# Folding the sub-key weights of a product-key expert layer: unreduced 32-bit products in two column tiles, the folded pieces kept on chip

## The chip, the cores and the metric

One core of a Trainium2 chip runs the kernel. The metric is the device time of one execution in microseconds (us). TensorE multiplies matrices, VectorE (DVE) and ScalarE (ACT) work on elements, GpSimd (POOL) too, and SyncE (SP) issues nearly all transfers, in the order of the program. Each engine takes its own instructions in order and waits on semaphores for the others. All data in fast memory lie in 128 partitions; products land in PSUM, in banks of 512 32-bit numbers for each partition.

## What is computed

Attention with 16 heads, and then a layer of experts that are found by product keys, each behind a layer norm and with a residual sum. N is 2048 tokens, D = 448.

```python
h  = x + attention(layernorm(x), wqkv, wo)
xf = layernorm(h)
q  = einsum("nd,dhc->nhc", xf, w_q)           # 16 heads, 2 x 256
s1 = einsum("nhd,ed->nhe", q[..., :256], k1)  # 64 sub-keys
s2 = einsum("nhd,ed->nhe", q[..., 256:], k2)
# the 8 best of each, the 8 best of their 64 sums, softmax g over these, for each head
act = gelu(einsum("nd,nhkd->nhk", xf, u[top_e]))
out = h + einsum("nhk,nhk,nhkd->nd", g, act, v[top_e])
```

The scores s1 and s2 depend on xf only through products of w_q with the sub-keys. The kernel forms those products once (the *folding*: for each head a matrix of 448 x 128, 64 columns for k1 and 64 for k2), and later multiplies xf with the folded matrix.

## The kernel before

**Stages.** First the layer norm and the projections to q, k and v (up to about 152 us). Then attention in 256 steps; a step u takes one block of 128 keys for four heads and 512 queries. Beside its steps run the folding, the preparation of u and v, and for three of the four blocks of 512 tokens the output projection (`project`) and the search for the best sub-keys (`search`). After it (from about 925 us) come the experts.

**Order.** The order of every engine's instructions is the program's. `weave` (L163) lays generators side by side: each gets a number of turns and a stretch, in attention steps, and the one whose next turn is due first goes next. So a stretch (1, 59) with 48 turns has one turn in 1.21 steps. What a function puts into `due` is issued at the next `flush` (L179), at the latest in the next attention step.

**An attention step.** `scores` issues twelve products for S, two steps ahead, and ScalarE takes two exponentials (L530). `values` (L546) multiplies V with the exponentials in four column tiles of 32, unreduced 32-bit on both sides, into the accumulator A. There is one bank named A: after 16 steps (u = 15, 31, ...) VectorE copies it out (L557), and the next accumulation may begin. Three steps later `finish` (L533) transposes the copy in four products (L540) and VectorE divides by the sums (L542, L543). Every fourth step, after its products with V, `load_kv` (L206) loads K and V for a group of four steps two groups later (L201, L213). There is also only one bank named M; the folding, `finish`, `project` and `search` all take it in turn.

**The folding** (class `Fold`, L225). The sub-keys are split into a high and a low part in the 32-bit form with reduced products, 64 columns each, side by side (`kk`). For each head h and half f, VectorE casts the raw weights to a high part (L252), and VectorE (f = 0) or GpSimd (f = 1) subtracts for the low part (L254). `fold` issues four products of 448 columns (through the helper at L90): two contraction tiles by the high and low part. VectorE copies the lower 64 rows out (L266) and adds the upper ones (L267), and fills the last 64 columns (L269). `flip` transposes the head's matrix in four products (L277), ScalarE copies it out (L279), and at the next flush VectorE takes the largest magnitude (L139 by `see`) and SP stores the piece to the slow memory (L283). Raw weights are loaded four heads ahead (L242), into eight buffers. That is three turns for a head.

**Scales and halves.** The folded weights, u and v are scaled by a power of two from their largest magnitude and split into two 16-bit parts, a pair that is called halves below. For u and v, `tops` (L969) loads each of 32 tiles and takes its maximum two turns later. `share` (L141) reduces the maxima (L142), writes 128 numbers to the slow memory (L144), reads them back for all partitions (L146), and VectorE reduces them (L149) and forms the scale. `part` (L982) then loads a tile (L984), makes its halves (for the folded weights on VectorE, L159 and L991; for u and v on GpSimd, L993 to L997) and stores them (L1000). The halves of two parts have five buffers, which u and the folded weights share.

**The stretches**, in attention steps of the whole: folding 1 to 59; maxima of u 1 to 25; scale of u 26 to 33; halves of u 33 to 59 (14 tiles) and 64 to 110 (18); scale of the folded weights 60 to 65, their halves 65 to 87; wo loaded 60 to 68; projections from 67, 131 and 195, each followed by its search 26 steps on; maxima of v 87 to 110, its scale 111 to 116, its halves 118 to 170 and 170 to 240.

Of the kernel before, what the change touches and what calls it, by code (L numbers as in the profile page):

```python
# [58 lines left out]
def block(ctx: ExitStack, tc: tile.TileContext, x, wqk, wv, wo, wq, k12, uT, v, cst, out):  # L59
# [4 lines left out]
    v_d = dram.tile([4, 4, 128, 4, 128], F32, name="vd")  # L64
    wr_d = [dram.tile([128, 4, 128], F32, name=f"wr{h}") for h in range(H)]
    wp_d = [dram.tile([128, 2, 4, 4, 128], F16, name=f"wp{i}") for i in range(4)]
# [156 lines left out]
    class Fold:  # L223


        def __init__(self, rawp):
            self.rawp = rawp
            kr = rawp.tile([128, 2, 2, 64], F32, name="kr", bufs=1)
            nc.sync.dma_start(kr, k12)
            self.kk = kk = rawp.tile([128, 2, 2, 128], FR, name="kk", bufs=1)  # L230
            nc.vector.tensor_copy(kk[:, :, :, :64], kr)
            nc.vector.tensor_tensor(kk[:, :, :, 64:], kr, kk[:, :, :, :64].bitcast(F32), op=OP.subtract)
            self.raw = {}
            for h in range(4):
                self.load(h)
# [9 lines left out]
        def run(self, pool, psum):  # L245

            parts, wts = {}, {}

            def parts_of(h, f):
                w = self.raw[h][f]  # L250
                wh = pool.tile([128, 2, D], FR, name="wqh", bufs=4)
                nc.vector.tensor_copy(wh, w)  # L252
                wl = pool.tile([128, 2, D], FR, name="wql", bufs=4)
                (nc.gpsimd if f else nc.vector).tensor_tensor(wl, w, wh.bitcast(F32), op=OP.subtract)  # L254
                parts[h, f] = wh, wl

            def fold(h, f):
                pf = psum.tile([128, 512], F32, name="M")
                hl = parts.pop((h, f))
                mm_all(pf[:, :D], [(self.kk[:, f, kt], r[:, kt]) for kt in range(2) for r in hl])  # L260

                def add():
                    if not f:
                        wts[h] = pool.tile([128, 512], F32, name="wt")
                    lo = pool.tile([64, D], F32, name="lo", bufs=1)
                    nc.vector.tensor_copy(lo, pf[64:, :D])  # L266
                    nc.vector.tensor_tensor(wts[h][64 * f:64 * f + 64, :D], pf[:64, :D], lo, op=OP.add)  # L267
                    if f:
                        nc.vector.tensor_copy(wts[h][:, D:], wts[h][:, 384:D])  # L269

                due.append(add)

            def flip(h):
                wt = wts.pop(h)
                pt = psum.tile([128, 4, 128], F32, name="M")
                for t in range(4):
                    nc.tensor.transpose(pt[:, t], wt[:, 128 * t:128 * t + 128], ident)  # L277
                of = pool.tile([128, 4, 128], F32, name="of")
                nc.scalar.activation(of, pt, AF.Copy)  # L279

                def store():
                    WS.see(h, of.rearrange("p t c -> p (t c)"))
                    nc.sync.dma_start(wr_d[h], of)  # L283

                due.append(store)

            parts_of(0, 0)
            parts_of(0, 1)
            for h in range(H + 1):
                for f in range(2):  # L290
                    if h < H:
                        flush()
                        fold(h, f)
                        if h + 1 < H:
                            parts_of(h + 1, f)
                            if f:
                                self.raw.pop(h)
                                self.load(h + 4)
                        yield
# [682 lines left out]
    def part(S, src, dst, cols, planes):  # L982
# [5 lines left out]
        r, h = raw[:, :cols], [hl[:, k, :cols] for k in range(planes)]  # L988
        if S is WS:
            times(h[0], r, S.scale)  # L990
            nc.vector.scalar_tensor_tensor(h[1], r, S.scale, h[0], op0=OP.mult, op1=OP.subtract)  # L991
        else:
            nc.gpsimd.tensor_scalar(r, r, S.scale, 1.0, op0=OP.mult, op1=OP.mult)  # L993
            nc.gpsimd.tensor_copy(h[0], r)
            nc.gpsimd.tensor_tensor(h[1], r, h[0], op=OP.subtract)
            if planes == 3:
                nc.gpsimd.tensor_scalar(h[2], h[0], 1.0 / LS, 1.0, op0=OP.mult, op1=OP.mult)  # L997
        yield
# [11 lines left out]

    def parts_of_folded():
        return pipeline([part(WS, wr_d[h].rearrange("p t c -> p (t c)"),
                              wp_d[h // 4][:, :, h % 4].rearrange("p f t c -> p f (t c)"), 512, 2) for h in range(H)], 1)

    def scales():
# [4 lines left out]
        yield  # L1020

    with tc.manual_schedule(engines={ET.PE, ET.DVE, ET.Activation, ET.Pool, ET.SP}):
# [24 lines left out]
        wol = wo_p.tile([128, 4, D], FR)  # L1047
        work = [(a, 197, 0, 197), (load_wo(), 5, 0, 8)]
        for b in range(3):
            t = 64 * b + 7  # L1050
            look = search(b, [(i, j) for g in ((0, 1), (2, 3)) for i in range(4) for j in g])
            work += [(project(b), PROJECT, t, t + PROJECT), (islice(look, 1), 1, t + 22, t + 23)]
            t += 26
            work += [(look, SEARCH, t, t + SEARCH)]
            if b < 2:
                work += [(chain(*[pairs_of(j, nc.gpsimd) for j in range(4)]), 4 * PAIRS_POOL, t + 18, t + 82),
                         (places_of(b, nc.scalar), PLACES, t + 82, t + 94)]
            else:
                work += [(pipeline([pairs_of(j, nc.gpsimd) for j in (0, 1)], 6), 6 + PAIRS_POOL, t + 20, 197)]
# [182 lines left out]
```

## Time and profile before

| | |
|---|---|
| median of three runs | 1704.33 us (1703.49 to 1708.09) |
| the profiled execution | 1696.69 us |
| its span, first to last instruction | 1694.9 us |
| mean granted clock of TensorE | 0.984 |
| moved by transfers | 301.32 MB, mean 178 GB/s |

In the rows that follow, a group names the line, the engine, the operation, what is written and read, the shape and the count; behind the bar stand the busy time in us and the mean of one in ns, then the idle time of the engine just before, and what ended it. A row of the chain has a start, a length and what it was spent on: the work of an engine, a transfer, or the issue of one on SP's queue (SPq). A row of a window has the stretch, its length, and the busy time of the engine with the count of instructions, then the granted clock, the share of the transfer engines and GB/s. A row of waits has the total in us, the count and the longest.

### The profile page before, as it was taken

Reading aid. Unit: us, or ns where it says so; the run is one execution under the profiler, and the core shown is the slowest. Engines: PE = TensorE matmul, PEld = TensorE weight load, DVE = VectorE, ACT = ScalarE, POOL = GpSimd, SP = SyncE. Lnnn points to the kernel's source line nnn. Section 1 sums busy time; section 2 is a strip of 40 time slices with the busy share of each in tenths; the row PEclk is TensorE's granted clock in tenths of the full one; section 3 lists DMA queues with packets and bytes.
Section 4 is the critical chain, followed back from the end, with each engine's and each line's share of the span. In section 5 each row is a group of like instructions: output and inputs, shape, how many; then the busy total and the mean of one; then the engine's idle time right before and its main releaser. Section 6 shows DMA issues by size and latency. Waiting matters only on the chain.

```text
span 1694.9 us, 33544 instructions
## 1 busy us (share of the span) xinstructions
PE 1598.7 (94%) x12577; PEld 811.4 (48%) x12577; DVE 1254.8 (74%) x3907; ACT 896.7 (53%) x1272; POOL 421.1 (25%) x514
## 2 busy tenths in 40 slices
PE   6999898987899999999998899899999999999999
PEld 5776343443333443344333564445544554555544
DVE  6654866456587658857678899968999799779832
ACT  3545666775677877688775344233432344333322
POOL 3452115634414663267534200000000000000000
PEclk9999999998999999999999999999999999999999
DMA  8755958678984666455752324445434443554354
GB/s 262 258 193 182 300 196 273 223 244 262 337 293 137 204 224 191 157 178 181 252 174 80 94 83 136 142 125 147 125 115 138 150 130 101 153 152 130 107 146 134
DMA packets 164356, 301.32 MB, mean 178 GB/s; under 512 B 15328, under 2 KB 63584, under 8 KB 164192
## 3 DMA queue, kind: packets, MB, share of 16 engines
q1 hardware_dynamic: 159968, 297.07, 55.7%
q10 hardware_dynamic: 4224, 2.10, 0.4%
q8 instruction: 99, 1.62, 0.4%
q14 instruction: 65, 0.53, 0.1%
HBM read 237.24 MB, written 61.87 MB: 176 GB/s over the span
## 4 chain that ended last, share of the span: by engine, by line
PE 62%; DVE 24%; DMA 8%; issue 2%; POOL 1%; ACT 1%; SPq 0%; DVEq 0%; POOLq 0%; ACTq 0%
PE acc L1157 15%; PE M L90 10%; PE A L90 9%; PE A L552 9%; PE S L526 9%; PE pq L90 6%; DVE p L932 4%; DVE ti L762 2%; DVE G L953 2%; DMA raw<-in_uT_dram 2%; DVE fg L917 2%; DVE pos L789 2%; DMA raw<-in_v_dram 1%; DVE ti L761 1%; PE A L959 1%
## 5 line engine op out<-in xcount | busy, mean ns | idle before, releaser
L530 ACT ACTIVATE P<-S 128x1024 f32<-128x1024 f32 x512 | 495.9, 1022 | 134.8 <-PE S L526 133.5
L1157 PE MATMUL acc<-v,w 128*128 128x448 f16 x1536 | 306.0, 353 | 0.0
L526 PE MATMUL S<-qS,kS 32*128 32x512 f32 x3072 | 267.0, 432 | 5.2 <-ACT P L530 4.5
L552 PE MATMUL A<-P,V 128*32 128x512 f32 x2048 | 267.8, 613 | 3.4 <-DVE o L557 3.4
L526 PEld LDWEIGHTS S<-qS,kS 32*128 32x128 f32 x3072 | 140.5, 186 | 161.6 <-issue 96.9
L1157 PEld LDWEIGHTS <-w 128*128 128x128 f16 x1536 | 149.0, 98 | 141.7 <-issue 1.4
L90 PEld LDWEIGHTS <-u 128*128 128x128 f16 x1408 | 133.5, 98 | 151.7 <-issue 11.1
L1131 ACT ACTIVATE w<-ring 128x512 f16<-128x512 f32 x128 | 80.5, 630 | 205.4 <-PE acc L1157 106.6
L932 DVE TENSOR_TENSOR p<-st,iota 128x2048 f16<-128x2048 f16 x128 | 156.4, 1222 | 7.7 <-PE A L959 4.1
L90 PE MATMUL A<-XHb,u 128*128 128x512 f16 x568 | 138.5, 388 | 4.5 <-DVE G L953 4.0
L90 PE MATMUL M<-w,XHb 128*128 128x512 f16 x512 | 129.8, 384 | 7.4 <-DMA w<-wp 3.1
L1132 DVE SCALAR_TENSOR_TENSOR w<-w,ring 128x512 f16<-128x512 f16 x128 | 87.2, 686 | 66.2 <-ACT w L1131 66.2
L1130 DVE SCALAR_TENSOR_TENSOR ring<-ring,wscale,G 128x512 f32<-128x512 f32 x128 | 92.7, 744 | 34.6 <-ACT ring L1116 34.4
L90 PE MATMUL M<-XHb,u 128*128 128x512 f16 x456 | 110.9, 379 | 0.8 <-DVE G L953 0.8
L552 PEld LDWEIGHTS A<-P,V 128*32 128x32 f32 x2048 | 45.9, 109 | 108.2 <-issue 99.6
L813 POOL TENSOR_TENSOR sel<-sel,iv 128x256 f16<-128x256 f16 x80 | 54.0, 706 | 174.1 <-DVE sel L809 174.1
L1116 ACT ACTIVATE ring<-A,ugelu 128x512 f32<-128x512 f32 x71 | 48.5, 684 | 89.2 <-PE A L90 89.1
L761 DVE MAX8 ti<-fresh 128x8 f32<-128x64 f32 x384 | 80.6, 210 | 17.1 <-ACT fresh L739 17.0
L762 DVE FIND_INDEX8 ti<-ti,fresh 128x8 uint32<-128x64 f32 x384 | 84.2, 219 | 0.0
L1116 ACT ACTIVATE ring<-M,ugelu 128x512 f32<-128x512 f32 x57 | 39.2, 688 | 81.9 <-PE M L90 81.7
L90 PEld LDWEIGHTS <-XHb 128*128 128x128 f16 x512 | 45.4, 98 | 72.5 <-issue 21.3
L917 DVE TENSOR_TENSOR fg<-f,st 128x2048 f16<-128x2048 f16 x64 | 78.7, 1230 | 0.1
(197 smaller groups left out, 2325.7 us busy)
## 6 DMA issues: line engine op xcount, KB each, us to landing
v<-vs SPq DMA_DIRECT2D x128, 336.0 KB, 2.9
kS<-ks SPq DMA_DIRECT2D x64, 512.0 KB, 5.5
u<-us SPq DMA_DIRECT2D x128, 256.0 KB, 2.7
w<-wp SPq DMA_DIRECT2D x56, 512.0 KB, 5.5
V<-vd SPq DMA_DIRECT2D x64, 256.0 KB, 3.1
raw<-in_uT_dram SPq DMA_DIRECT2D x64, 256.0 KB, 5.1
wr<-in_wq_dram SPq DMA_DIRECT2D x32, 448.0 KB, 6.3
raw<-in_v_dram SPq DMA_DIRECT2D x64, 224.0 KB, 5.3
```

The source lines that it names most:

```text
L90: nc.tensor.matmul(ps, l, r, start=i == 0, stop=i == len(pairs) - 1)
L526: nc.tensor.matmul(S[j // 2][:, j % 2], kS[r, a, 128 * (k % 4):128 * (k % 4) + 128], qS[r, c], start=m == 0, stop=m == 2)
L530: nc.scalar.activation(Pt[:, 2 * i:2 * i + 2], S[i], AF.Exp)
L552: nc.tensor.matmul(O[n][32 * j:32 * j + 32], V[:, k % 4, j], Pt[:, j], start=k == 0, stop=k == NT - 1)
L761: nc.vector.max(t8[:, 4 * i + k], src[:, 64 * k:64 * k + 64])
L762: nc.vector.max_index(i8[:, 4 * i + k], t8[:, 4 * i + k], src[:, 64 * k:64 * k + 64])
L917: nc.vector.tensor_tensor(fg.rearrange("p t k f u -> p t k (f u)"), f1.rearrange("p t f u -> p t (f u)").unsqueeze(2).to_broadcast([128, T ...
L932: newest[0] = nc.vector.tensor_tensor(p1, pairs(0, s, TG, 128), ids(TG, 128), op=OP.is_equal).ins
L1116: nc.scalar.activation(act, p, AF.Gelu_apprx_tanh, scale=ugelu)
L1130: nc.vector.scalar_tensor_tensor(av, av, wscale, of_expert(b, f), op0=OP.mult, op1=OP.mult)
L1132: nc.vector.scalar_tensor_tensor(w[:, 1], w[:, 0], -LS, a, op0=OP.mult, op1=OP.add)
L1157: nc.tensor.matmul(acc[j][:, :D], l, r, start=f == 0 and k == 0, stop=f == 31 and k == 2)
```

## The change

The raw weights and sub-keys are multiplied as they are, unreduced 32-bit on both sides. Each head has one turn with four products: two contraction tiles, and in each the two halves f as two column tiles of 64, into the two halves of one bank. No cast, no subtraction and no sum is left; VectorE copies the 128 x 448 out and fills the last 64 columns. A head takes two turns (fold, flip); the raw weights of head h + 4 are loaded right behind the fold of head h. ScalarE copies each flipped piece to a tile of its own, which stays; the store and the load of the pieces go. `Fold.parts` makes the halves from these tiles.

The first stretch of the weave grows from 60 to 66 steps. In it: folding 1 to 50 in 32 turns; then, in one chain, the scale of the folded weights and their halves, 51 to 66, in 21 turns; maxima of u as before; scale of u 26 to 32; the first 14 halves of u 32 to 66. Behind it, in steps of the whole: wo 66 to 71, the other 18 halves of u 66 to 106, maxima of v 72 to 132 (60 steps instead of 23), its scale 133 to 139, its halves 140 to 186 (14 tiles) and 186 to 246 (18). The first loads of each search come two steps earlier. Projections and searches stay where they were.

```diff
-            kr = rawp.tile([128, 2, 2, 64], F32, name="kr", bufs=1)
-            nc.sync.dma_start(kr, k12)
-            self.kk = kk = rawp.tile([128, 2, 2, 128], FR, name="kk", bufs=1)
-            nc.vector.tensor_copy(kk[:, :, :, :64], kr)
-            nc.vector.tensor_tensor(kk[:, :, :, 64:], kr, kk[:, :, :, :64].bitcast(F32), op=OP.subtract)
+            self.keys = rawp.tile([128, 2, 2, 64], F32, name="kr", bufs=1)
+            nc.sync.dma_start(self.keys, k12)
...
-            def fold(h, f):
+            def fold(h):
                 pf = psum.tile([128, 512], F32, name="M")
-                hl = parts.pop((h, f))
-                mm_all(pf[:, :D], [(self.kk[:, f, kt], r[:, kt]) for kt in range(2) for r in hl])
-
-                def add():
-                    if not f:
-                        wts[h] = pool.tile([128, 512], F32, name="wt")
-                    lo = pool.tile([64, D], F32, name="lo", bufs=1)
-                    nc.vector.tensor_copy(lo, pf[64:, :D])
-                    nc.vector.tensor_tensor(wts[h][64 * f:64 * f + 64, :D], pf[:64, :D], lo, op=OP.add)
-                    if f:
-                        nc.vector.tensor_copy(wts[h][:, D:], wts[h][:, 384:D])
+                w = self.raw.pop(h)
+                for kt in range(2):
+                    for f in range(2):
+                        nc.tensor.matmul(pf[64 * f:64 * f + 64, :D], self.keys[:, f, kt], w[f][:, kt],
+                                         start=kt == 0, stop=kt == 1)
+
+                def out():
+                    wts[h] = pool.tile([128, 512], F32, name="wt")
+                    nc.vector.tensor_copy(wts[h][:, :D], pf[:, :D])
+                    nc.vector.tensor_copy(wts[h][:, D:], pf[:, 384:D])
...
-                of = pool.tile([128, 4, 128], F32, name="of")
-                nc.scalar.activation(of, pt, AF.Copy)
-
-                def store():
-                    WS.see(h, of.rearrange("p t c -> p (t c)"))
-                    nc.sync.dma_start(wr_d[h], of)
+                of = pool.tile([128, 512], F32, name=f"of{h}", bufs=1)
+                nc.scalar.activation(of, pt.rearrange("p t c -> p (t c)"), AF.Copy)
+                self.folded.append(of)
+                due.append(lambda: WS.see(h, of))
...
-        STEPS = 3 * H
+        STEPS = 2 * H
+
+        def parts(self):
+
+            for h, of in enumerate(self.folded):
+                hl = sp.tile([128, 2, 512], F16, name="hl", tag="hl2", bufs=5)
+                times(hl[:, 0], of, WS.scale)
+                nc.vector.scalar_tensor_tensor(hl[:, 1], of, WS.scale, hl[:, 0], op0=OP.mult, op1=OP.subtract)
+                yield
+                nc.sync.dma_start(wp_d[h // 4][:, :, h % 4].rearrange("p f t c -> p f (t c)"), hl)
...
-        weave((islice(a, 60), 60, 0, 60), (fold[0].run(fold_p, P[0]), Fold.STEPS, 1, 59),
-              (tops(US, lambda f: uT[:, f].rearrange("p t e -> p (t e)"), 512), TOPS, 1, 25), (US.share(), 5, 26, 33),
-              (parts_of_up(0, 14), 14 + PART, 33, 59))
+        weave((islice(a, FOLDED), FOLDED, 0, FOLDED), (fold[0].run(fold_p, P[0]), Fold.STEPS, 1, 50), (chain(WS.share(), fold[0].parts()), 5 + H, 51, FOLDED),
+              (tops(US, lambda f: uT[:, f].rearrange("p t e -> p (t e)"), 512), TOPS, 1, 25), (US.share(), 5, 26, 32),
+              (parts_of_up(0, 14), 14 + PART, 32, FOLDED))
...
-        work += [(WS.share(), 5, 0, 5), (parts_of_folded(), H + PART, 5, 27), (parts_of_up(14, 32), 18 + PART, 4, 50),
-                 (tops(VS, lambda f: v[:, f], D), TOPS, 27, 50), (VS.share(), 5, 51, 56), (scales(), 1, 56, 57),
-                 (parts_of_down(0, 14), 14 + PART, 58, 110), (parts_of_down(14, 32), 18 + PART, 110, 180)]
+        work += [(parts_of_up(14, 32), 18 + PART, 0, 40), (tops(VS, lambda f: v[:, f], D), TOPS, 6, 66), (VS.share(), 5, 67, 73), (scales(), 1, 73, 74),
+                 (parts_of_down(0, 14), 14 + PART, 74, 120), (parts_of_down(14, 32), 18 + PART, 120, 180)]
```

More of the change, by code (lines that the diff above doesn't have):

```diff
@@ L277, in flip @@
                     nc.tensor.transpose(pt[:, t], wt[:, 128 * t:128 * t + 128], ident)
[L278 to L299 removed]
+                of = pool.tile([128, 512], F32, name=f"of{h}", bufs=1)
+                nc.scalar.activation(of, pt.rearrange("p t c -> p (t c)"), AF.Copy)
+                self.folded.append(of)
+                due.append(lambda: WS.see(h, of))
+            for h in range(H + 1):
+                if h < H:
+                    flush()
+                    fold(h)
+                    self.load(h + 4)
+                    yield
                 if h:
@@ L988, in part @@
         r, h = raw[:, :cols], [hl[:, k, :cols] for k in range(planes)]
[L989 to L997, printed above, removed]
+        nc.gpsimd.tensor_scalar(r, r, S.scale, 1.0, op0=OP.mult, op1=OP.mult)
+        nc.gpsimd.tensor_copy(h[0], r)
+        nc.gpsimd.tensor_tensor(h[1], r, h[0], op=OP.subtract)
+        if planes == 3:
+            nc.gpsimd.tensor_scalar(h[2], h[0], 1.0 / LS, 1.0, op0=OP.mult, op1=OP.mult)
         yield
@@ L1020, in scales @@
         yield
+    FOLDED = 66
     with tc.manual_schedule(engines={ET.PE, ET.DVE, ET.Activation, ET.Pool, ET.SP}):
```

24 lines of the change are left out of this document (7 added, 17 removed).

## The prediction

> **What bounds the kernel now.** I read the page first, then a table of stretches for the exponentials of the attention, then the chain of waits, the groups by shape, and the waits of SP's queue.
>
> ```profile
> PE 1598.7 (94%) x12577; PEld 811.4 (48%) x12577; DVE 1254.8 (74%) x3907; ACT 896.7 (53%) x1272; POOL 421.1 (25%) x514
> PE 62%; DVE 24%; DMA 8%; issue 2%; POOL 1%; ACT 1%; SPq 0%; DVEq 0%; POOLq 0%; ACTq 0%
> ```
>
> The page shows TensorE busy for 94% of the span, but only 62% of the chain is its; VectorE holds 24% and transfers 8%. So TensorE is made to wait somewhere, and the change is worth what it does to those places. The next table finds them. Its rows are stretches in us; the count is that of exponentials, two to an attention step, so each stretch is known in steps (26, 24, 16, then six steps of the third again, 36, 24 and 36).
>
> ```profile
> core 0: us, ACT busy (x), PEclk, DMA share, GB/s
> 153.30:235.50 82.20, 50.39 (x52) 0.94 0.79 261
> 235.50:304.30 68.80, 46.53 (x48) 1.00 0.69 232
> 304.30:345.60 41.30, 31.02 (x33) 1.00 0.60 190
> 333.50:345.60 12.10, 11.62 (x13) 1.00 0.49 126
> 345.60:467.30 121.70, 69.70 (x72) 0.93 0.86 294
> 467.30:542.80 75.50, 46.52 (x48) 1.00 0.69 222
> 550.90:649.50 98.60, 69.69 (x72) 1.00 0.67 212
> ```
>
> A step with nothing beside it takes 12.1/6 = 2.02 us. Steps 66 to 102 (from 345.6) and their counterpart 64 steps later (from 550.9) issue the same work on TensorE, a projection and the start of a search, yet the first takes 121.7 us against 98.6: 23.1 us more, at a granted clock of 0.93 and a DMA share of 0.86. The folding runs beside steps 1 to 59, and its floor follows from the chain where nothing disturbs it:
>
> ```profile
> 288.85 0.59 PE M L277 x4
> 289.43 0.91 PE S L526 x11
> 290.34 0.99 PE A L552 x8
> 291.34 1.01 PE M L90 x4
> ...
> 310.99 0.67 PE M L540 x4
> ```
>
> A step is S and A, 1.90 us; a half fold (four products) adds 1.01, a flip (four transposes) 0.59. A head has two half folds and a flip in 58/16 = 3.625 steps: 2 x 2.91 + 2.49 + 0.625 x 2.02 = 9.57 us, 153.1 for 16. With two plain steps and three finishes of an accumulator (0.67 each, the last row) steps 0 to 60 would take 159 us. They took 192.3 - 12.1 = 180.2 (the first three rows less the fourth). So 21 us are stalls, about 13 of them in the first row: its floor is 25/3.625 x 9.57 + 2.0 + 0.7 = 68.7 of 82.2.
>
> **The change, part by part.** *Products.* Four products with 128 output columns per half become four products per head with 64, in unreduced 32-bit form. The nearest rows are V times P: unreduced too, four column tiles of 32.
>
> ```profile
> 461.11 1.85 PE A L552 x16
> L552 PE MATMUL A<-P,V 128*32 128x512 f32 x648 | 88.9, 621 | 1.7 <-DVE o L557 1.7
> ```
>
> A step has four such products and the trace shows eight instructions, so each product is two passes. Sixteen instructions in 1.85 us are four slots of 0.46 us in which the four tiles run side by side. For 448 columns a slot is 0.46 x 448/512 = 0.405 us; two contraction tiles by two passes make four slots if the two column tiles overlap: 1.62 us, and 0.07 at the edge (0.99 alone against 0.925 in the row of sixteen): 1.69 per head against 2.02. The trace has no column tile of 64, so both ends: 1.62 if they overlap, and 8 x 0.62 x 448/512 = 4.34 us if every pass waits for the one before and lasts as long as its record. I take 1.69, as the row of A is nearest. A faster order than A's is excluded, since passes into one half of the bank follow one another.
>
> The Trainium skill ("TensorE: Matmul & The Clock Gate", Part 3, The mechanism) says that matmuls start and end strictly in program order. If the two passes of a product stand side by side in that order, the second tile could begin only with the first one's second pass: five slots, 2.03 us per head, 6.5 us more. For A that would be five slots of 0.46 = 2.3 us a step; the trace has 0.99, so it speaks against it here.
>
> A head now has one fold and one flip in 49/16 = 3.06 steps: (1.90 + 1.69) + 2.49 + 1.06 x 2.02 = 8.22 us, 131.5 for 16. That is steps 1 to 50; with step 0, three finishes and 16 plain steps, steps 0 to 67 have a floor of 131.5 + 2.0 + 2.0 + 32.3 = 167.8, against 194.3 measured (192.3 and one plain step).
>
> *VectorE and GpSimd.* Per head the casts, one subtraction, the two copies and two sums go; the other subtraction leaves GpSimd (16 x 2.13 us, off the chain).
>
> ```profile
> L254 POOL TENSOR_TENSOR wql<-wr,wqh 128x896 fp32r<-128x896 f32 x16 | 34.0, 2127 | 112.5 <-DVE wqh L252 53.6 <-PE M L90 35.3 <-issue 17.5
> L266 DVE COPY lo<-M 64x448 f32<-64x448 f32 x32 | 20.0, 626 | 25.9 <-PE M L90 25.2
> L267 DVE TENSOR_TENSOR wt<-M,lo 64x448 f32<-64x448 f32 x32 | 19.7, 617 | 1.1
> L254 DVE TENSOR_TENSOR wql<-wr,wqh 128x896 fp32r<-128x896 f32 x15 | 19.4, 1295 | 0.5
> L252 DVE CAST wqh<-wr 128x896 fp32r<-128x896 f32 x29 | 19.2, 662 | 0.0
> L269 DVE COPY wt<-wt 128x64 f32<-128x64 f32 x16 | 7.4, 465 | 0.5
> L139 DVE TENSOR_REDUCE tops<-of 128x1 f32<-128x512 f32 x16 | 11.0, 685 | 24.0 <-ACT of L279 24.0
> L557 DVE COPY o<-A 128x512 f32<-128x512 f32 x5 | 3.4, 687 | 7.3 <-PE A L552 7.3
> ```
>
> Before: 2 x (0.63 + 0.62 + 0.66) + 1.30 + 0.47 + 0.69 = 6.3 us a head. After: one copy of 128 x 448 (not in the trace; 0.63 to 0.69 by the copies of 64 x 448 and 128 x 512), one of 64 columns and the maximum: 1.7 to 1.8. So 4.5 us a head, 72 us in all, leave an engine that is in order and whose evacuation of the one bank M is what the next fold or flip waits for.
>
> ```profile
> 169.86 6.62 DMA raw<-in_uT_dram
> ...
> wr<-in_wq_dram SPq DMA_DIRECT2D x32, 448.0 KB, 6.3
> ...
> SPq L283 <- ACT of L279: 53.3, 13, 6.4
> SPq L213 <- PE A L552: 36.6, 12, 8.5
> ```
>
> These are a row of the chain, one of the page's table of transfers and two of the waits of SP's queue between 153 and 330 us. The stalls of the first row begin here: tiles of u arrive late, the maximum over them holds VectorE, and the evacuation behind it holds TensorE. They arrive late because SP's queue stands still for the store of each folded piece (53.3 us). These stores go. In their place the load of head h+4 waits until TensorE has finished fold h, since the raw weights are now read there; behind it in SP's queue are its own 0.9 MB (two of 448 KB, 3.5 us at the 261 GB/s of the first row) and the next tiles of u, whose maxima VectorE then awaits, 3 to 4 us a head. But the evacuation stands ahead of those maxima, and VectorE has the slack to catch up. Bounds for the stalls left up to step 51: nothing, or all 21. I take 8, since transfers still move about as many bytes in this stretch (each head's pieces no longer go out, but more heads come in).
>
> *Sharing the scale and making the halves, now beside steps 51 to 66.* It was at steps 60 to 87. What the maximum's round trip takes and two of the halves, from the timeline, and both kinds of halves, grouped between 345.6 and 467.3 us:
>
> ```profile
> 334.48 0.16 DVE L142 TENSOR_REDUCE top<-tops 128x1 f32<-128x16 f32 x1
> 337.48 0.38 SPq L144 DMA_DIRECT2D topw<-top  x1
> 345.11 0.32 SPq L146 DMA_DIRECT2D every<-topw  x1
> 350.46 0.28 DVE L149 TENSOR_REDUCE top<-every 128x1 f32<-128x128 f32 x1 [4.76 <-DMA every<-topw]
> ...
> 402.41 0.48 DVE L159 TENSOR_SCALAR hl<-raw,scale 128x512 f16<-128x512 f32 x1
> 402.93 0.75 DVE L991 SCALAR_TENSOR_TENSOR hl<-raw,scale,hl 128x512 f16<-128x512 f32 x1
> ...
> L991 DVE SCALAR_TENSOR_TENSOR hl<-raw,scale,hl 128x512 f16<-128x512 f32 x16 | 14.6, 911 | 0.6
> L159 DVE TENSOR_SCALAR hl<-raw,scale 128x512 f16<-128x512 f32 x16 | 11.4, 710 | 20.5 <-DMA us<-hl 14.5 <-DMA wp<-hl 5.9
> ```
>
> From the first reduction to the scale are 16.8 us, eight plain steps. Issued at step 51.4, it is done near step 59.6, but the first halves stand in the program at step 54.9 and one more every 0.71 step. VectorE starts them 17.3 us after step 51 begins and needs 0.91 + 0.71 = 1.62 us each. At step 63 it must copy the attention's accumulator out of its only bank; twelve halves stand ahead of it: 17.3 + 12 x 1.62 + 0.7 = 37.4 us, where TensorE wants the bank for step 64 at 13 x 2.02 + 1 = 27.2. So a new stall of 10 us. The remaining four halves (6.5 us) pass while TensorE does steps 64 to 66. Upper bound: add the 20.5 us that these lines waited for buffers of earlier stores; lower: none of that, and with each half at 0.48 + 0.75 us, the shortest of them, the stall is 17.3 + 14.8 + 0.7 - 27.2 = 5.6. I take 10.
>
> Steps 0 to 67: 167.8 + 8 + 10 = 185.8 against 194.3: **8.5 us gained**.
>
> *Steps 66 to 102.* The sixteen halves (26 us of VectorE, and the 20.5 of waiting), sixteen loads of pieces and sixteen stores leave, as do the first tiles of v, whose maxima waited for their landing:
>
> ```profile
> L139 DVE TENSOR_REDUCE tops<-raw 128x1 f32<-128x448 f32 x16 | 9.6, 612 | 18.5 <-DMA raw<-in_v_dram 18.5
> ```
>
> These are now one in 1.8 steps instead of 0.7, so their transfers have time. The 23.1 us of excess should shrink to what the remaining preparation of u (denser by one in seven) and the loads of wo cost; bounds are 0 and 23, I take 5: **18 us gained**.
>
> *Later.* VectorE's search gets eleven percent more work in steps 110 to 126 (0.61 us in 1.8 steps) and loses the wait of sharing v's scale; together nothing, covered by the gaps of steps 102 to 110. That sharing (a round trip like the above) moves to steps 133 to 139, where steps are short and the second projection needs VectorE: it comes some 5 us late there (16.8 us against 4.8 steps of 2.3 to 2.5), and I charge **4 us** (0 to 7), with the denser halves of v on GpSimd, which still has idle time (25% busy), in it.
>
> Sum: 8.5 + 18 - 4 = 22.5 us. The profiled execution took 1696.69 us (span 1694.9 and 1.8 around it); that would become 1674. The median of the three runs shown is 1704.33, 7.6 above; I take the change off that: **1682**.
>
> **The rivals.** *The column tiles take turns* (slower). If the two tiles of 64 do not overlap, a head's fold costs between eight slots, 3.24 us, and 4.34; that is 1.6 to 2.65 more, 26 to 42 over 16 heads, every one on TensorE, which then bounds steps 1 to 50. It decides against the change from 22.5/16 = 1.4 us a head. Middle: 34, so 1716. For it: no tile of 64 is in the trace. Against: the four tiles of 32 do overlap.
> *Five slots*, by program order: 1682 + 6.5 = 1688.5; A's rows speak against it.
> *The new stall is larger*: the halves wait for buffers as they did (20.5 us, of which half in front of the copy): 1692. For it: five buffers shared with u's halves, in a shorter time.
> *The stall of steps 66 to 102 is u's and wo's*: two thirds of the 23.1 stay, gain 8 there, and the new stall comes on top, eating the rest: 1682 + 10 + 8 = 1700, no measurable change. For it: these transfers remain, and GpSimd waited for tiles of u in that stretch (the row below); against: VectorE's wait of 20.5 us is that of the removed lines.
>
> ```profile
> POOL raw L993 <- DMA raw<-in_uT_dram: 18.7, 4, 7.3
> ```
>
> *All stalls up to step 51 go*, and the halves run at their shortest: 8 + 4 less, 1670.
>
> **How the numbers follow.** About 0.3% (5 us) is what a measurement can tell from no change. Chances: forecast 0.46 (own range 1675 to 1690), five slots 0.04, larger stall 0.14, stalls gone 0.10: faster 0.74. Excess stays 0.14: within. Tiles in turn 0.12: slower. The range 1669 to 1706 leaves out the last of these cases and little else.
>
> **What would show it.** The products of a fold of one head should span about 1.7 us (right) or over 3 (tiles in turn). SP's wait for the folded piece must be gone, with waits of the loads of wq for TensorE in its place. TensorE should stand about 10 us before step 64 for the copy of the accumulator, and steps 66 to 102 should take 104 us or less. VectorE should be some 70 us less busy, and 8 MB less moved. I am wrong if the fold's stretch still stalls by 20 us with VectorE half idle: then transfers alone bounded it.

## The result and the profile after

The median of seven runs is 1697.82 us, of seven runs of the kernel before 1704.33: a ratio of 0.9955 with an interval of 0.9941 to 0.9969. So the change gains 0.45%, 6.5 us between the medians, of the 22 that were forecast. The direction held, and the time lies in the wide range of 1669 to 1706, but not in the forecast's own range of 1675 to 1690: the size did not hold. The profiled execution took 1694.8 us, its span is 1693.0. The two profiles are only 1.9 us apart, since the one before was 7.6 us below its median and the one after 3.0 below; what follows is read from these two.

One row of the page after, the busy time of the engines:

```profile
PE 1598.3 (94%) x12577; PEld 803.2 (47%) x12577; DVE 1174.7 (69%) x3809; ACT 896.5 (53%) x1272; POOL 381.7 (23%) x498
```

VectorE has 80 us less to do (1254.8 before), GpSimd 39, and 8.4 MB less were moved (292.92 against 301.32). The work that was meant to go is gone. Hardly any of it is seen in the time, and a table by stretches says where it went. The stretches begin and end with the same attention steps in both kernels: 0, 32, 34, 66, 68, 72, 74, 102 and 126. After:

```profile
154.20:244.40 90.20, 61.75 (x64) 1.00 0.77 264
244.40:258.30 13.90, 3.90 (x5) 0.85 0.45 172
258.30:336.40 78.10, 61.90 (x64) 0.98 0.52 174
336.40:357.50 21.10, 3.94 (x6) 0.60 0.77 235
357.50:366.90 9.40, 7.72 (x8) 1.00 0.91 287
366.90:385.40 18.50, 3.91 (x5) 0.63 0.32 104
385.40:464.50 79.10, 54.17 (x56) 1.00 0.88 299
464.50:540.10 75.60, 46.54 (x49) 1.00 0.62 203
```

Before, the same steps:

```profile
153.30:251.10 97.80, 61.99 (x64) 0.95 0.74 244
251.10:256.70 5.60, 3.92 (x5) 1.00 0.02 8
256.70:345.60 88.90, 62.03 (x65) 1.00 0.73 240
345.60:349.60 4.00, 3.87 (x4) 1.00 0.13 48
349.60:361.40 11.80, 7.76 (x9) 1.00 1.04 386
361.40:367.60 6.20, 3.79 (x4) 1.00 0.79 232
367.60:467.30 99.70, 54.28 (x57) 0.91 0.88 297
467.30:542.80 75.50, 46.52 (x48) 1.00 0.69 222
```

Each row has the stretch, its length, ScalarE's busy time with the count of instructions, the granted clock, the share of the transfer engines and GB/s. Four stretches got shorter, by 7.6, 10.8, 2.4 and 20.6 us: 41 us together. Three stretches of two steps each got longer, by 8.3, 17.1 and 12.3: 38 us. Those three are new stalls. The difference, 3.6 us with the last row, is all that is left at step 126; the experts' stage, whose program is the same, gives 2.5 of the lead back in this one profile. In the rows of the three new stalls the granted clock is 0.85, 0.60 and 0.63, against 1.00 in the same steps before; in the longest of the four that got shorter it is 1.00 for 0.91.

What each is, is told by the waits of the kernel after between 320 and 380 us, and by its timeline:

```profile
DVE top L148 <- DMA every<-topw: 16.5, 1, 16.5
PEld A L536 <- DVE o L541: 14.9, 1, 14.9
PE A L536 <- DVE o L541: 14.4, 1, 14.4
...
DVE woh L573 <- DMA wor<-in_wo_dram: 13.2, 4, 4.5
DVE hl L158 <- DMA wp<-hl: 10.0, 4, 4.1
```

```profile
253.88 0.28 DVE L148 TENSOR_REDUCE top<-every 128x1 f32<-128x128 f32 x1 [10.72 <-DMA every<-topu]
...
254.65 0.61 DVE L255 COPY wt<-M 128x448 f32<-128x448 f32 x1
...
255.54 1.08 PE L264 MATMUL M<-ct,wt 128*128 128x128 f32 x4 [6.45 <-DVE wt L256]
...
309.19 0.16 DVE L141 TENSOR_REDUCE top<-tops 128x1 f32<-128x16 f32 x1
...
325.83 0.29 DVE L148 TENSOR_REDUCE top<-every 128x1 f32<-128x128 f32 x1 [16.49 <-DMA every<-topw]
...
350.25 0.68 DVE L541 COPY o<-A 128x512 f32<-128x512 f32 x1
...
360.51 0.56 SPq L577 DMA_DIRECT2D wor<-in_wo_dram  x1
...
377.95 0.74 PE L89 MATMUL M<-woh,oh 128*128 128x448 f32 x1 [3.55 <-DVE woh L573]
```

**Steps 32 and 33**: VectorE awaits the scale of u (10.72 us) with the evacuation of a fold behind it in its order (`wt`, L255), and TensorE's flip waits for that (6.45 us). **Steps 66 and 67** (by the exponentials, which run two steps ahead; TensorE stands before the products with V of step 64): VectorE awaits the scale of the folded weights for 16.5 us, then makes twelve halves from 326.8 to 350.2, and only then copies the accumulator out of its one bank. **Steps 72 and 73**: the first tile of wo is asked for at 360.5 us; the projection's first products need all four, which come through two buffers one after the other, and the last one is cast at 377.5. In the kernel before the four came through two buffers as well, and steps 72 and 73 took 6.2 us; there the first was asked for at 337.0 us, 24 us ahead of step 72, and here 6 us ahead.

### The profile page after: what moved, and what is told of

It is laid out like the page before. It is cut to its first block, busy times and chain, and to the rows that moved or that the text cites. A ratio compares the mean times of both kernels' runs of the same rounds, so it can differ in the third digit from the quotient of the medians.

```text
span 1693.0 us, 33318 instructions
## 1 busy us (share of the span) xinstructions
PE 1598.3 (94%) x12577; PEld 803.2 (47%) x12577; DVE 1174.7 (69%) x3809; ACT 896.5 (53%) x1272; POOL 381.7 (23%) x498
## 2 busy tenths in 40 slices
DMA packets 159748, 292.92 MB, mean 173 GB/s; under 512 B 14817, under 2 KB 63073, under 8 KB 159585
## 4 chain that ended last, share of the span: by engine, by line
PE 66%; DVE 18%; DMA 8%; issue 3%; POOL 3%; ACT 1%; SPq 1%; DVEq 0%; POOLq 0%
PE acc L1134 15%; PE M L89 11%; PE A L536 10%; PE S L510 9%; PE A L89 9%; PE pq L89 6%; DVE p L916 4%; DVE G L937 2%; DMA raw<-in_uT_dram 2%; DVE ti L746 2%; DVE fg L901 1%; DMA w<-wp 1%; DVE pos L773 1%; PE A L943 1%; PE M L118 1%
## 5 line engine op out<-in xcount | busy, mean ns | idle before, releaser
L89 PEld LDWEIGHTS <-u 128*128 128x128 f16 x1408 | 133.4, 98 | 151.5 <-issue 10.8
L1108 ACT ACTIVATE w<-ring 128x512 f16<-128x512 f32 x128 | 80.5, 629 | 205.1 <-PE acc L1134 109.9
L973 POOL TENSOR_SCALAR raw<-raw,scale 128x512 f32<-128x512 f32 (+1 forms) x64 | 46.8, 731 | 178.8 <-DMA raw<-in_uT_dram 166.3
```

The costliest lines, as they stand in the source:

```text
L89: nc.tensor.matmul(ps, l, r, start=i == 0, stop=i == len(pairs) - 1)
L1108: nc.scalar.activation(w[:, 0], a, AF.Copy, scale=1.0 / LS)
```

## The experiments

The theory after this reading: the products and the halves kept on chip are worth about 40 us, and three separate waits, each made by *where* a step was put and not by what it does, take most of it back. The rivals: one backlog of VectorE that shows in three places; the transfers at their limit; or the moved stretches of v. Each of twelve kernels was timed beside the kernel before on the same chip. The median of the kernel before was 1701.6 to 1705.9 in these rounds, so runs of different rounds are compared by their ratios.

| run | median, us | ratio to before, interval |
|---|---|---|
| only_products | 1685.99 | 0.9906 (0.9880 to 0.9931) |
| only_spread | 1710.38 | 1.0051 (1.0025 to 1.0077) |
| f_outer | 1695.73 | 0.9949 (0.9933 to 0.9965) |
| early_wo | 1686.02 | 0.9907 (0.9873 to 0.9942) |
| late_u_scale | 1689.90 | 0.9918 (0.9894 to 0.9943) |
| own_ring | 1692.88 | 0.9933 (0.9899 to 0.9966) |
| early_scale | 1697.73 | 0.9962 (0.9947 to 0.9977) |
| load_behind | 1692.54 | 0.9950 (0.9932 to 0.9967) |
| three | 1674.41 | 0.9842 (0.9815 to 0.9868) |
| three_v | 1681.87 | 0.9881 (0.9847 to 0.9915) |
| four | 1672.02 | 0.9813 (0.9777 to 0.9850) |
| five | 1669.00 | 0.9793 (0.9754 to 0.9831) |

One caution on single profiles: most of these runs have the same program up to step 26 as the kernel after, and took 73.9 to 80.5 us for it. Differences of a few us in these steps of one profile are noise.

### The parts alone

**only_products**: the kernel before with the fold of the kernel after, and nothing else.

```diff
-                mm_all(pf[:, :D], [(self.kk[:, f, kt], r[:, kt]) for kt in range(2) for r in hl])
+                for kt in range(2):
+                    for f in range(2):
+                        nc.tensor.matmul(pf[64 * f:64 * f + 64, :D], self.keys[:, f, kt], w[f][:, kt],
+                                         start=kt == 0, stop=kt == 1)
...
-        STEPS = 3 * H
+        STEPS = 2 * H
```

> Only the products: the kernel before with the fold of the kernel after (unreduced products, two column tiles, no casts, subtractions and sums), the pieces still stored and loaded again, stretches and all later work as before. Theory (VectorE relieved): step 60 is reached 8 to 12 us earlier, as in the kernel after, and the whole gets 8 to 12 us faster; the other 7 us lost in the kernel after come from what was moved. Rival (queue): with the store of the pieces kept and the new wait of the loads for TensorE added, SP's queue stands longer and step 60 is reached no earlier.

Measured: 0.9906, 16 us, where 8 to 12 were expected. The products alone gain more than the whole change. The stretches are steps 0 to 66 and 66 to 102, first the kernel before (it took 192.3 and 121.7), then two rows of this run:

```profile
153.30:345.60 192.30, 175.16 (x1513) 76.44 (x1514) 118.37 (x192) 135.98 (x149) 74.04 (x66) 0.97 0.71 235
...
153.60:330.10 176.50, 171.05 (x1516) 64.98 (x1514) 49.80 (x101) 135.59 (x148) 37.54 (x51) 0.98 0.80 257
330.10:453.10 123.00, 104.63 (x856) 45.46 (x857) 70.17 (x177) 78.51 (x89) 50.27 (x59) 0.92 0.86 290
```

TensorE's busy time stands first, VectorE's third. Steps 0 to 66 are 15.8 us shorter with VectorE at 49.8 us instead of 118.4, although the store of each piece stays in SP's queue and the loads of raw weights now wait for TensorE. TensorE's products between 153 and 345 us, one row of the kernel before and two of this one, show what it waited for:

```profile
L90 PE MATMUL M<-wqh,kk 128*128 128x448 f32 x64 | 26.8, 418 | 13.7 <-DVE wt L267 13.2 <-DVE ob L543 0.4
...
L251 PE MATMUL M<-wr,kr 128*64 128x448 f32 x128 | 27.6, 552 | 0.1
L265 PE MATMUL M<-ct,wt 128*128 128x128 f32 x64 | 10.9, 295 | 2.6 <-DVE wt L257 2.5
```

TensorE stood 13.7 us before the folds, nearly all of it for VectorE's sums (L267), and now 0.1, with 2.6 before the flips (1.4 in the kernel before). The shorter products (1.66 us a head for 2.02) give 5.8 us more. So VectorE's work on the fold was the greater part of what held these steps, and the queue was less than the prediction made of it; whether its whole load counts or only the copies that free the bank M is not separated. Steps 66 to 102 are as long as before, so the products have no part in their excess.

**only_spread**: the kernel before with v's stretches of the kernel after.

```diff
-(tops(VS, lambda f: v[:, f], D), TOPS, 27, 50), (VS.share(), 5, 51, 56), (scales(), 1, 56, 57),
-                 (parts_of_down(0, 14), 14 + PART, 58, 110), (parts_of_down(14, 32), 18 + PART, 110, 180)]
+(tops(VS, lambda f: v[:, f], D), TOPS, 12, 72), (VS.share(), 5, 73, 79), (scales(), 1, 79, 80),
+                 (parts_of_down(0, 14), 14 + PART, 80, 126), (parts_of_down(14, 32), 18 + PART, 126, 186)]
```

> Only the stretches of v: the kernel before with the maxima of v in steps 72 to 132, its scale at 133 to 139, its halves at 140 to 186 and 186 to 246, as in the kernel after; all else as before. Theory (the removed halves of the folded weights were the excess of steps 66 to 102): those steps gain 5 us or less, as VectorE's 18 us of waiting for v were mostly covered. Rival (v was the excess): they gain 10 to 18 us of the 23. Either way the later scale of v costs 4 us or less at steps 133 to 139.

Measured: 1.0051, slower, by less than 1%. Neither theory nor rival: steps 66 to 102 took 126.8 us against 121.7, and 102 to 126 79.7 against 75.5.

```profile
PE M L119 <- DVE ob L543: 10.5, 1, 10.5
DVE hl L159 <- DMA raw<-in_uT_dram: 8.2, 1, 8.2
DVE tops L139 <- DMA raw<-in_v_dram: 7.4, 3, 5.0
```

In these waits between 410 and 470 us VectorE still waits for v, and it stands for more besides, once with TensorE behind it for 10.5 us. A possible reading is that loads of v, spread among the halves of the folded weights, lengthen the queue for both; no run shows it. That the spread alone gains nothing fits the theory's view that the 18.5 us for which VectorE waited for v before were mostly covered.

**f_outer**: the kernel after with the loops over f and the contraction tiles exchanged, so that in the program both products of one column tile come before both of the other.

```diff
-                for kt in range(2):
-                    for f in range(2):
+                for f in range(2):
+                    for kt in range(2):
```

> The kernel after with the four products of a fold in another order: both contraction tiles of half 0, then both of half 1, so that the column tiles no longer alternate in the program. Theory (each column tile is fed by itself): nothing changes, 1.65 us for a head's eight passes. Rival (program order: a pass starts no earlier than the one before it): only the last pass of half 0 meets the first of half 1, seven slots of 0.38 us, 2.6 to 2.8 us for a head, 16 us more on TensorE in steps 1 to 50, of which at least 8 are seen at step 50.

The groups of these products between 153 and 345 us, in the kernel after and in this one:

```profile
L250 PE MATMUL M<-wr,kr 128*64 128x448 f32 x128 | 27.6, 552 | 1.6 <-issue 1.6
```

```profile
L250 PE MATMUL M<-wr,kr 128*64 128x448 f32 x128 | 27.7, 552 | 2.2 <-issue 2.2
```

128 passes of 552 ns each, in 27.6 and 27.7 us: eight passes in 1.73 us by the group, 1.66 between neighbours in the chain, in either order. The whole is the same as well, 0.9949 against 0.9955. The two column tiles run side by side whichever way the program names them. Whether the order is mended on the way to the engine or each tile of the array is fed by itself, the trace cannot tell.

### The three waits, one by one

**early_wo**: wo is loaded at steps 46 to 50, in two transfers, into buffers of the search that are still free.

```diff
+    def fetch_wo():
+        for g in range(2):
+            raw_wo.append(sp.tile([128, 2, 512], F32, name="wor", tag="w", bufs=3))
+            nc.sync.dma_start(raw_wo[g][:, :, :D], wo[:, 2 * g:2 * g + 2])
+            yield
...
-                prev = w2.tile([128, 512], F32, name="wor", tag="xt")[:, :D]
-                nc.sync.dma_start(prev, wo[:, g])
+                prev = raw_wo[g // 2][:, g % 2, :D]
```

> wo is loaded at steps 46 to 50 into buffers that the search uses later, instead of from step 66 on, one step ahead of the first projection; casts and subtractions stay at step 66. Theory (lead): steps 72 and 73 together took 18.5 us since the first product of the projection waited for wo; they take 6 to 8, and the whole gets 10 to 12 us faster. Rival (backlog): VectorE's halves and GpSimd's order hold the casts anyway: 4 us or less gained.

Measured: 0.9907 against 0.9955, 8 us by the ratios and 12 by the medians. Steps 72 and 73 in its profile:

```profile
367.00:373.30 6.30, 6.30 (x51) 3.33 (x46) 1.43 (x3) 4.44 (x6) 3.82 (x6) 1.00 0.39 139
```

6.3 us instead of 18.5, all of it busy TensorE, and the gain lasts to the end (span 1680.3 against 1693.0). The theory of the lead holds; the backlog is no part of it. The edit also gives all four tiles of wo a place at once; the kernel before, with two buffers and a lead of seven steps, shows that the lead is enough.

**late_u_scale**: `(US.share(), 5, 26, 38)` for `(US.share(), 5, 26, 32)`, and the first halves of u in 38 to 66.

> The scale of u is shared in steps 26 to 38 instead of 26 to 32, the first 14 halves of u follow in 38 to 66 instead of 32 to 66. Theory: steps 32 and 33 took 13.9 us since VectorE awaited the scale's round trip with the fold's evacuation behind it; they take 6, and up to step 50 8 us are gained. Rival: the halves of u, denser now, hold more of the shared buffers after step 54, the stall before step 64 grows by 5 us or more and eats most of it.

Steps 32 and 33 take 6.2 us instead of 13.9, and the wait for the accumulator's copy grows:

```profile
PE A L536 <- DVE o L541: 22.1, 1, 22.1
DVE top L148 <- DMA every<-topw: 17.1, 1, 17.1
```

from 14.4 to 22, as the rival had it, and 28.1 us for steps 66 and 67. So 7.7 us are gained at steps 32 and 33 and 7.0 lost at steps 66 and 67. But steps 32 to 102 together took 215.0 us against 220.1, and over the rounds the run is 0.9918 against 0.9955: the stall grew as the rival said, and it did not eat most of the gain. Together with the next edit the growth is gone (7.5 us of waiting in three).

**own_ring**: the halves of the folded weights get eight buffers in the folding's pool.

```diff
-                hl = sp.tile([128, 2, 512], F16, name="hl", tag="hl2", bufs=5)
+                hl = fold_p.tile([128, 2, 512], F16, name="hlw", bufs=8)
```

> The halves of the folded weights get eight buffers of their own in the folding's pool instead of sharing five with the halves of u. Theory (order): the stall before step 64 is VectorE's order, a late scale and twelve halves ahead of the accumulator's copy; waits for buffers are only 7 us of it, so the 14 us for which TensorE waits for that copy fall to 7 or 8, and the whole gets 6 us faster. Rival (buffers): the stores' landing sets the pace of the halves; the stall falls to 2 us or less, the whole gets 13 us faster. A third (transfers): the wait moves to SP's queue or to GpSimd, and nothing is gained.

```profile
PE A L536 <- DVE o L541: 10.2, 1, 10.2
```

14.4 us became 10.2, where 7 or 8 were expected; in the whole, 0.9933 against 0.9955 is within the intervals. The waits of VectorE for stores are gone, and a late scale with twelve halves behind it is still there: the buffers were 4 us, the rest is order and the halves themselves. The twelve took 19.6 us (23.5 in the kernel after) with hardly any wait (0.4 us), and not 12 x (0.48 + 0.75) = 14.8, since VectorE's instructions were longer where GpSimd worked beside them:

```profile
331.52 1.22 POOL L975 TENSOR_TENSOR hl<-raw,hl 128x512 f16<-128x512 f32 x1
331.75 1.53 DVE L289 SCALAR_TENSOR_TENSOR hlw<-of,scale,hlw 128x512 f16<-128x512 f32 x1
...
337.56 0.75 DVE L289 SCALAR_TENSOR_TENSOR hlw<-of,scale,hlw 128x512 f16<-128x512 f32 x1
```

In this run, L289 took 0.75 us where GpSimd stood still, and 1.11 on average where GpSimd worked for more than half of its time. So making the halves of u in the same steps costs VectorE time even where no buffer is shared.

**early_scale**: folding 1 to 41, scale 41.5 to 53, halves 53 to 66, with the shared buffers.

> Folding in steps 1 to 41 instead of 1 to 50, the scale of the folded weights shared in 41.5 to 53, its halves in 53 to 66. Theory (order): the round trip no longer stands between VectorE and the halves, so the accumulator's copy at step 63 comes on time: the 14 us of waiting fall to 4 or less, 10 us faster. Rival (buffers): halves at the same pace of 1.9 us each still are 10 us late at step 63: 4 us or less gained. Rival (transfers): with more heads in steps 1 to 25, the loads of raw weights and tiles of u collide and those steps get 5 us longer or more.

No gain over the kernel after (0.9962 against 0.9955), and the rival of the buffers is what the profile shows. The scale came nearly on time (VectorE waited 1.6 us for it), and still the wait for the copy stayed (14.3 us), as the halves were no faster: their waits between 320 and 372 us are

```profile
DVE hl L158 <- DMA us<-hl: 10.3, 3, 4.4
DVE hl L158 <- DMA wp<-hl: 6.3, 5, 2.1
```

An earlier scale without buffers of its own buys nothing. The rival of the transfers stays open: step 32 was reached 111.6 us after step 0 instead of 90.2, but this profile is the slowest of the run's eleven executions (1705.5, median 1697.7).

**load_behind**: `self.load(h + 3)` for `self.load(h + 4)`, behind the fold of head h.

> The raw weights are loaded three heads ahead instead of four, so that their buffers were read by the fold of the head before, and SP's queue need not stand until TensorE has finished the fold just issued (38 us of waiting between 155 and 242 us). Theory (queue): the tiles of u behind these loads land earlier, VectorE's wait for them (35 us) falls below 15 us, and steps 0 to 28 are 5 us shorter, as is the whole. Rival (transfers at their limit): the wait for u stays within 5 us of what it was and the steps gain 1 us or nothing.

SP's queue between 155 and 242 us, first the kernel after, then this one:

```profile
SPq L238 <- PE M L250: 38.5, 10, 12.8
```

```profile
SPq L212 <- PE A L536: 31.2, 7, 5.9
SPq L238 <- PE M L250: 9.2, 1, 9.2
```

The wait for the fold is gone but for one time, and about half of it passed to the loads of V, which wait for TensorE as well (14.7 us in the kernel after). VectorE's wait for u fell from 34.8 to 22.0 us, and step 28 came 77 us after step 0 instead of 80, within the noise of these steps. In the whole the ratio is 0.9950 against 0.9955, which is no difference that these rounds can show; as the fourth edit below it is 0.9813 against 0.9842, within the intervals too. It is inconclusive.

### Together

**three**: early_wo, own_ring and late_u_scale. **three_v**: the same with v's stretches of the kernel before. **four**: three and load_behind. **five**: four, with the folding in 1 to 45, its scale in 45 to 56, its halves in 56 to 66.

> Three edits together: wo loaded at steps 46 to 50, eight own buffers for the halves of the folded weights, the scale of u shared in steps 26 to 38. Theory (three separate waits): the gains add: 12 us for wo, 4 for the buffers, and the 8 us at steps 32 and 33 that the denser halves of u took away before are now kept: 1674 to 1680 us, at step 104 some 25 us ahead of the kernel before. Rival (one chain, VectorE's backlog): each edit uncovers the next wait, and it is no better than the earlier wo alone, 1684 to 1688.

> The kernel with three edits (wo earlier, own buffers, later scale of u; 1674 us), and v's stretches put back to where they were before the change: maxima in steps 87 to 110, scale 111 to 116, halves 118 to 170 and 170 to 240. Theory (spreading v costs, as it did alone, since its loads and maxima then meet the projection of steps 67 to 92): steps 72 to 104 get some us faster, the whole 2 to 6 us faster. Rival (with the halves of the folded weights gone from steps 65 to 87 the spread has room, and packed maxima wait for their tiles as they did, 18 us): 5 us or more slower.

> The kernel with three edits and also the raw weights loaded three heads ahead instead of four. Theory (queue): the 3 to 4 us that this gave at steps 28 to 60 on its own add: 1670 to 1672 us. Rival: the wait moves to the next sharing of a scale or to VectorE's copy before step 64: within 1.5 us of 1674.

> The kernel with four edits, and the folding in steps 1 to 45 instead of 1 to 50, the scale of the folded weights shared in 45 to 56, its halves in 56 to 66, so that VectorE's wait for the round trip ends before the halves are due. Theory (order): with own buffers a half takes 1.3 to 1.6 us, and the wait of 7.5 us for the accumulator's copy before step 64 falls below 3; 4 to 6 us faster than with four. Rival (density): folding in 44 steps costs the steps up to 28 as much or more, as in the run with 40 steps, and the whole is no faster.

Three reaches 1674.41, 0.9842 against 0.9955: 19 us by the ratios, where the three edits alone gave 8, 4 and 6. The gains add, so the waits were three and not one. Putting v's stretches back costs 7 us by the ratios (4.6 between the profiled spans, 1678.0 and 1673.4; the intervals overlap), with this wait of VectorE between 345 and 470 us:

```profile
DVE tops L138 <- DMA raw<-in_v_dram: 26.1, 8, 7.2
```

So the spread of v, which cost when the halves of the folded weights shared its steps, probably pays once they have left. This run also divides the gain of steps 74 to 102: with v as before and the halves gone they took 87.0 us, against 99.7 in the kernel before and 81.0 in three. About 13 us are then the halves', and some 6 the spread's, if the earlier wo and scale have no part in these steps. Four and five are the fastest, 0.9813 and 0.9793. In five the last wait, which was expected to fall below 3 us, did not:

```profile
DVE top L148 <- DMA every<-topw: 9.2, 1, 9.2
PE A L536 <- DVE o L541: 8.9, 1, 8.9
```

VectorE still waits 9.2 us for the scale: it came 22.1 us after its reduction (283.0 to 305.1 us in this trace), and VectorE's turn for it 12.9 us after. Then thirteen halves stood ahead of the copy and took 25.3 us, 1.95 each and not 1.3 to 1.6, with hardly a wait (0.5 us together) and GpSimd at work beside most of them. What gain five has over four lies before that, in steps 34 to 66 (74.6 us against 78.7), and it is within the intervals. It has the lowest median, 36.9 us below the kernel before by the medians of the same chip.

## Why the prediction was right and wrong

The step that failed is the size of the stalls that remain. The prediction's sum holds three of them, 8 + 10 + 5 = 23 us; by the profiles they were about 14, 16 and 13, together 44. In the terms of its sum: the 8.5 us gained in steps 0 to 67 became 6.2 lost (200.4 us against 194.2), the 18 in steps 67 to 102 became 9.9, the minus 4 later became minus 1, and step 0 began 0.9 later. That makes the 1.9 us between the two profiles. A small part is a slip: the floor for steps 0 to 67 counts 16 plain steps behind step 50 where there are 17, so 167.8 should be 169.8.

*The products.* Right: 1.69 us for a head were forecast, 1.66 measured, and the column tiles of 64 overlap as those of 32 do. "Tiles in turn" and "five slots" are refuted by the group of 128 passes; by the order of the loops too, as far as the program's order reaches the engine. The rule of the Trainium skill that was weighed ("TensorE: Matmul & The Clock Gate", Part 3, The mechanism), read as a strict order of the passes in the program, would have shown in f_outer above all, and did not.

*Stalls up to step 51.* "I take 8": too low, and named for the wrong cause. Steps 0 to 50 took 149.0 us (154.2 to 303.2) where the prediction's floor for them is 134.8 (131.5, a plain step and two finishes), so about 14 are left, and 8.3 of these are one event at steps 32 and 33, the sharing of u's scale, 26 to 32 instead of 26 to 33. The text gave this stretch in the list of changes and priced nothing for it; in only_products, with the same products and the old stretch, these two steps took 4.6 us. The store in SP's queue, which the prediction blamed, was not what mattered most: with it kept, only_products gained 15.8 us by step 66. Nor was it the wait for tiles of u: between 155 and 242 us VectorE waited 9.0 us for them before and 34.8 after, and these steps got shorter all the same.

*The new stall before step 64.* "I take 10": mechanism right, size short (14.4 us of waiting, and steps 50 to 67 took 51.4 us, 16.4 above a floor of 17 plain steps and a finish). The copy was done 45.7 us after the start of step 51 (303.2 + 2.0 to 350.9) and not 37.4. The round trip began 3.3 us after its turn, behind the division of the last accumulator, and took 17.4 us for 16.8; the twelve halves took 23.5 us for 19.4, 7.0 of them waits, most for the five buffers, which the prediction had as its upper bound and left out of its middle.

*Steps 66 to 102.* "I take 5" for what remains: too low by 8, and by a mechanism that the prediction does not have. Its own sign, 104 us or less, failed: they took 128.1. Without the two new stalls these steps took 9.4 + 79.1 = 88.5 us against 111.5 before, 23 less, more than the 18 forecast. But the load of wo had been put behind the longer first weave, from step 60 to step 66, with the projection still at 67: a lead of one step instead of seven. The prediction listed "the loads of wo" among small things that remain, without asking what they are late for; it cost 12.3 us, and early_wo took it back (6.3 us against 6.2 before).

*Later.* Minus 4 was forecast; from step 102 to the end of attention nothing was lost (2.9 us ahead at step 102, 4.4 at the end, counted from the start of the span). The scale of v at steps 133 to 139 cost nothing: steps 126 to 139 took 30.1 us in both kernels.

So of the rivals the one on a larger new stall came true, beside one that was not on the list: a load that lost its lead because the border of a stage moved. The rival at 1700 came nearest in number and named wo, but as a transfer that stays slow, together with u's, over the whole stretch; outside the two stalls that stretch gained more than forecast, so its number is luck. Without the stall for wo and the one at steps 32 and 33 the lead at step 126 would have been about 24 us (3.6 + 12.3 + 8.3), near the forecast of 22.5. That is partly luck too, since a larger stall before step 64 and larger gains behind it cancel.

## What to carry to other kernels

When a change moves the border between two stages, list every load that stands behind the border and count the steps between it and its first use, before and after: an unchanged line of code can lose its lead. Price a round trip through slow memory (here 16.6 us from the reduction to the value, and 22.1 in five) against the turns it is given, and look what stands behind the waiting instruction on its engine, in particular the one that frees an only bank. And when much work disappears and little time with it, cut both traces at the same steps of the program: a table of equal stretches shows at once whether nothing was gained or whether it was gained and given back.

## What the runs showed of the hardware that was not expected

Eight passes of unreduced 32-bit products of 448 columns in two column tiles took 1.66 us in either order of the program. The same VectorE instruction on 128 x 512 elements (L289) took 0.75 us alone and 1.11 on average where GpSimd worked for more than half of its time (own_ring). The same transfers cost differently by their neighbours: v spread over 60 steps cost 0.5% beside the halves of the folded weights, and packed again cost about 0.4% once these were gone (three_v against three; their intervals overlap).
